# Three moves in an instruction order: a merge behind the next maximum, a norm ahead of a merge, a product begun within another

## The chip, the cores and the metric

The kernel runs on one core of one Trainium2 chip. The metric is the device time of one execution in microseconds (us), lower is better. The time before is 416.09 us, the median of 6 runs (415.14 to 417.43).

## The reference

Attention with normalised queries and keys, and behind it a two-layer network without a bias:

```python
# q, k, v: (8, 12, 448, 64) float32; w_in (768, 2048), w_out (2048, 768)
def rmsnorm(x, g):
    return x / np.sqrt(np.mean(x * x, axis=-1, keepdims=True) + 1e-06) * g
q_n, k_n = rmsnorm(q, g_q), rmsnorm(k, g_k)
scores = (q_n @ k_n.transpose(0, 1, 3, 2)) / np.sqrt(64)
scores = scores - np.max(scores, axis=-1, keepdims=True)
attn = np.exp(scores)
attn = attn / (np.sum(attn, axis=-1, keepdims=True) + 1e-09)
x = (attn @ v).transpose(0, 2, 1, 3).reshape(3584, 768)
h = x @ w_in
out = np.maximum(0.01 * h, h) @ w_out
```

## The kernel before

**Units.** The attention is cut into 24 units `u`, each of four heads of one batch entry; three units make one batch entry `b` (448 tokens). A unit has four steps `d` = 0 to 3, each with one or two of its seven score tiles `t`. In a step TensorE (PE) makes the scores (`qk`, L199), ScalarE (ACT) takes their exponential (`ex`, L218), and PE multiplies with v one unit later (`pv`, L367, with the sums `zcol`, L307).

**The shift.** One constant per unit is subtracted inside the exponential. At `d` = 0 VectorE (DVE) takes the maximum of the first score tile (`shift_max`, L236) and multiplies it into a diagonal `dg` (L238). PE spreads it over the partitions with two small matmuls (`shift_mm`, L248). DVE reduces that (L249) to the bias `eb` (L257). The matmuls stand in PE's order behind the `pv` and `zcol` matmuls of the unit before; their result lies in the same PSUM tile as that unit's `pv`, which ACT copies out after L249 (`pv_out`, L322). Then come the exponential and on PE the items of the network.

**The norm of a later unit.** At `d` = 2 of unit `u`, unit `u + 2` is normalised: ACT makes `rinv` (L164, L165), DVE multiplies q by it and then k (`prep_norm`, both L171: `n<-rq`, `n<-rk`), and a transposing DMA on SP's queue (L183) reads the result.

**The product on GpSimd.** In some units `attn @ v` times 1/sum is taken on GpSimd (POOL): `xmul_pool`, L347, `xt<-x,rz`. It waits for `rz`, which four DMAs on SP's queue (L337) spread over the partitions.

**The network.** Its work is a list of items, `queue`, filled once per batch entry (`push`). A step pops as many items as the table `PLAN` says. Between items `fill` runs small pieces of attention work, the `jobs` of the step, one behind each item. First-layer items (`moe1`, L389) make 128 of the 2048 hidden features and end with the leaky ReLU on ACT (L383). Most second-layer tiles are made two at a time with Strassen's scheme, seven products instead of eight (`seven`, items `i0` to `i6`, all matmuls at L476). Each product is eight matmuls into a PSUM bank: `ma`, `mb`, `mc`, `md`. Two of them are used twice: the sixth product (`i5`) adds into `mc`, the seventh (`i6`) into `md`, each after DVE has read what the third-bank and fourth-bank products (`i3`, `i4`) left there. DVE merges the products into the output tile `ost` (`add`, L483; the first is a copy, L496), and `put` stores it through SP's queue (L409). The operands `sa` are sums of hidden features that DVE makes (`s1` to `s4`, L457 to L466).

**Order.** There is no scheduler: each engine runs its instructions in the order in which the Python code issues them. A merge isn't issued with its product but put on the list `pend` by `later`; the next item's `flush` issues what is on the list. At the end of a step `flush(keep=...)` issues it too, but may keep the sums `s1` to `s4` for the next step. `i4` carries a mark `merges`: behind it `fill` runs no job at `d` = 2, so that the norm doesn't stand before the merge of `i4`.

A group of seven products ends exactly at `d` = 3 of units 9, 12, 15, 18 and 21. There `i3` and `i4` lie in `d` = 2, `i5` and `i6` in `d` = 3, and the next unit's maximum follows.

**The tail.** Behind the attention come the last batch entry's items. The last group but one of seven products is `mixed`: its `sa` sums are made in two halves of four of the eight blocks, the second halves only when the last hidden features are there. So its `i0` makes six matmuls of `ma`, four of `mb` (first half of `sa` 1), and the last two of `ma`; `i1` makes the other four of `mb`.

Of the kernel before, what the change touches and what calls it, by code (L numbers as in the profile page):

```python
# [18 lines left out]
def kernel(  # L19
# [37 lines left out]
    def aux(shape, dtype, name):  # L57
        if held:
            return held[0].pop(0)
        return psum.tile(shape, dtype, tag="aux", bufs=4, name=name)  # L60
# [6 lines left out]
    def drop(bank):  # L67
        if held:
            held[0].append(bank)
# [24 lines left out]
    HF = FT // 2  # L94
    HC = DM // 2
    tw = cst.tile([P, 4, HF, HC], FP16)
    sa = cst.tile([P, 4, HF, P], FP16)
# [302 lines left out]
    def col(t):  # L400
        return 64 * (5 - 2 * t) if t < 3 else P * (t - 3)

    def store(pair, t, tile_, c, last):
        for y in range(2):
            n = 2 * t + (1 - y if t < 3 else y)
            b, grp = 2 * pair + n // NS, n % NS
            dst = out[b * S:(b + 1) * S, :].rearrange("(p t) m -> p t m", t=NS)
            eng = nc.scalar if last and y else nc.sync
            eng.dma_start(dst[:, grp, c], tile_[64 * y:64 * y + 64, c])  # L409

    ost = {}
    pend = []
    L, R, LR = slice(0, HC), slice(HC, DM), slice(0, DM)

    def flush(keep=False):
        kept = [p for p in pend if keep and p[0] in (s1, s2, s3, s4)]
        now = [p for p in pend if p not in kept]
        pend[:] = kept
        for fn, args in now:
            fn(*args)  # L420

    def out_tile():
        return opool.tile([P, DM], FP32, tag="ost", name="ost")

    def moe2(pair, t, half, part, late=False):
        flush()
        if half == 0 and part == 0:
            ost[0] = out_tile()
        if part == 0:
            ost[1] = aux([P, 512], FP32, "op2")  # L430
        op2 = ost[1]
        fts = (0, 1, 2, 3, 4, 5, 8, 9, 10, 12, 13, 11, 14, 15, 6, 7) if late else range(FT)
        for i in range(8 * part, 8 * part + 8):
            ft = fts[i]
            nc.tensor.matmul(op2[:, 0:HC], gt[:, ft, ds(col(t), P)], wout16[:, ft, ds(HC * half, HC)],  # L435
                             start=(i == 0), stop=(i == FT - 1))
        if part == 0:
            return
        nc.vector.tensor_copy(ost[0][:, ds(HC * half, HC)], op2[:, 0:HC])
        drop(op2)  # L440
        if half == 1:
            store(pair, t, ost[0], LR, False)

    def wblock(i, j):
        return wout16[:, HF * i:HF * i + HF, HC * j:HC * j + HC]
# [7 lines left out]
    def gblock(t, j):  # L453
        return gt[:, HF * j:HF * j + HF, ds(col(t), P)]
# [13 lines left out]
    def later(fn, *args):  # L468
        pend.append((fn, args))

    def seven(pair, tt, nxt=None, last=False, mixed=False):
        g = {}

        def mm(bank, a, b, first, fs=range(HF)):
            for f in fs:
                nc.tensor.matmul(bank[:, 0:HC], a[:, f], b[:, f], start=(first and f == 0), stop=(f == HF - 1), skip_group_check=not first)  # L476

        def bank(name):
            g[name] = aux([P, 512], FP32, name)
            return g[name]  # L480

        def add(dst, src, name):
            nc.vector.tensor_tensor(dst, g[name][:, 0:HC], src, op=ALU.add)  # L483

        def put(i, c):
            store(pair, tt[i], g["o"][i], c, last)

        def i0():
            flush()
            g["o"] = (out_tile(), out_tile())  # L490
            ma = bank("ma")
            if mixed:
                mm(ma, gblock(tt[0], 0), wblock(0, 0), True, range(6))
                mm(bank("mb"), sa[:, 1], tw[:, 1], True, range(4))
            mm(ma, gblock(tt[0], 0), wblock(0, 0), True, range(6 if mixed else 0, HF))
            later(lambda: nc.vector.tensor_copy(g["o"][1][:, L], g["ma"][:, 0:HC]))  # L496

        def i1():
            flush()
            mm(g["mb"] if mixed else bank("mb"), sa[:, 1], tw[:, 1], True, range(4 if mixed else 0, HF))  # L500
            later(lambda: add(g["o"][1][:, L], g["o"][1][:, L], "mb"))
            later(lambda: drop(g["mb"]))

        def i2():
            flush()
            mm(g["ma"], gblock(tt[0], 1), wblock(1, 0), False)
            later(lambda: nc.scalar.copy(g["o"][0][:, L], g["ma"][:, 0:HC]))
            later(lambda: drop(g["ma"]))
            if last:
                later(put, 0, L)  # L510

        def i3():
            flush()
            mm(bank("mc"), sa[:, 0], tw[:, 0], True)
            later(lambda: add(g["o"][1][:, R], g["o"][1][:, L], "mc"))
            if nxt:
                later(s1, nxt)

        def i4():
            flush()  # L520
            mm(bank("md"), sa[:, 2], tw[:, 2], True)
            later(lambda: add(g["o"][1][:, R], g["o"][1][:, R], "md"))
            if last:
                later(put, 1, R)

        i4.merges = True

        def i5():
            flush()
            mm(g["mc"], sa[:, 3], wblock(1, 1), False)  # L530
            if nxt:
                later(s2, nxt)
            later(lambda: add(g["o"][0][:, R], g["o"][1][:, L], "mc"))
            later(lambda: drop(g["mc"]))
            later(put, 0, R if last else LR)
            if nxt:
                later(s3, nxt)
                later(s4, nxt)

        def i6():  # L540
            flush()
            mm(g["md"], gblock(tt[1], 1), tw[:, 3], False)
            later(lambda: add(g["o"][1][:, L], g["o"][1][:, L], "md"))
            later(lambda: drop(g["md"]))
            later(put, 1, L if last else LR)

        return [i0, i1, i2, i3, i4, i5, i6]

    HK = KT // 2
# [191 lines left out]
    def fill(u, d, jobs):  # L741
        for n in range(int(PLAN[u - 3][d])):
            fn = queue.pop(0)[1]
            fn()
            if jobs and not (d == 2 and hasattr(fn, "merges")):
                jobs.pop(0)()
        flush(keep=d == 3 and u < NU - 1)
        for job in jobs:
            job()
# [21 lines left out]
    with tc.manual_schedule():  # L771
# [191 lines left out]
        for u in range(3, NU):  # L963
            for d in range(4):
# [24 lines left out]
                jobs = []  # L989

                def job(fn, *args):
                    jobs.append(lambda: fn(*args))
# [58 lines left out]
                if d == 3 and 6 <= u < NU - 3:  # L1051
                    for ti in range(2):
                        job(prep_sq, u + 3, ALL, (ti,))
                fill(u, d, jobs)
        zsum_slot(NU - 1)
        pv(NU - 1)
        zinv(NU - 1)
        xmul(NU - 1, (0,))
        for i, more in enumerate((((xmul, NU - 1, (1,)), (x_sum, B - 1, 3), (x_sum, B - 1, 1)), ((x_sum, B - 1, 2), (x_sum, B - 1, 4)))):
            c, fn = queue[i]  # L1060
# [33 lines left out]
```

## Time and profile before

| | us |
|---|---|
| median of 6 runs | 416.09 |
| lowest, highest run | 415.14, 417.43 |
| the profiled execution | 416.73 |
| its span (first to last instruction) | 414.9 |
| PE busy in it | 399.8 |
| DVE busy | 309.4 |
| ACT busy | 300.2 |
| POOL busy | 68.9 |

A row of the busy time by stretches has the stretch, its length, and then for PE, PE's weight loads, DVE, ACT and POOL the busy time and in brackets the number of instructions; then the granted TensorE clock (1.00 is full speed), the DMA engines' share and GB/s. A row of the order of time has the start and the duration in us, the engine, the line, the operation, `output<-inputs`, shapes and count, and in square brackets how long the engine sat idle before it and what ended that. Matmuls are pipelined: a row of eight matmuls of 384 columns is 1.46 us long, but the next product starts 1.30 us after it.

### The profile page before, as it was taken

Reading aid. Unit: us, or ns where it says so; the run is one execution under the profiler, and the core shown is the slowest. Engines: PE = TensorE matmul, PEld = TensorE weight load, DVE = VectorE, ACT = ScalarE, POOL = GpSimd, SP = SyncE. Lnnn points to the kernel's source line nnn. Section 1 sums busy time; section 2 is a strip of 40 time slices with the busy share of each in tenths; the row PEclk is TensorE's granted clock in tenths of the full one; section 3 lists DMA queues with packets and bytes.
Section 4 is the critical chain, followed back from the end, with each engine's and each line's share of the span. In section 5 each row is a group of like instructions: output and inputs, shape, how many; then the busy total and the mean of one; then the engine's idle time right before and its main releaser. Section 6 shows DMA issues by size and latency. Waiting matters only on the chain.

```text
span 414.9 us, 9374 instructions
## 1 busy us (share of the span) xinstructions
PE 399.8 (96%) x3831; PEld 219.8 (53%) x3831; DVE 309.4 (75%) x492; ACT 300.2 (72%) x470; POOL 68.9 (17%) x70
## 2 busy tenths in 40 slices
PE   8789999999999999999999999998999999999995
PEld 7455444554445544554445544454445557558863
DVE  5888798998788666767669757766768788658762
ACT  5898987677887699686987779866986657653600
POOL 1868432200020200020020100003002202000000
PEclk9899999999999999999999999999999999999999
DMA  6999999899665895678664795676662470032023
GB/s 203 277 236 253 240 250 163 214 177 207 136 155 96 222 236 91 154 174 185 154 154 75 211 214 131 171 155 122 201 112 47 120 148 20 8 78 76 2 56 98
DMA packets 71951, 62.41 MB, mean 150 GB/s; under 512 B 36325, under 2 KB 67045, under 8 KB 71909
## 3 DMA queue, kind: packets, MB, share of 16 engines
q1 hardware_dynamic: 61312, 49.62, 47.1%
q0 software_dynamic: 10272, 11.80, 18.2%
q8 instruction: 30, 0.49, 0.5%
q10 hardware_dynamic: 324, 0.39, 0.3%
q14 instruction: 13, 0.10, 0.1%
HBM read 45.61 MB, written 11.01 MB: 136 GB/s over the span
## 4 chain that ended last, share of the span: by engine, by line
PE 81%; DVE 9%; ACT 4%; issue 2%; DMA 2%; SPq 1%; DVEq 0%; ACTq 0%
PE hps L389 27%; PE sT L199 9%; PE op L435 5%; PE sT L367 5%; PE bank L602 5%; PE bank L476 5%; PE ma L476 5%; PE mc L476 4%; PE md L476 4%; DVE n L171 4%; ACT et L218 3%; PE mb L476 2%; PE zc L307 2%; PE sT L476 1%; DVE sT L236 1%
## 5 line engine op out<-in xcount | busy, mean ns | idle before, releaser
L218 ACT ACTIVATE et<-sT,eb 128x896 f16<-128x896 f32 x166 | 159.7, 1010 | 24.6 <-PE sT L199 14.6
L389 PE MATMUL hps<-xt,win 128*128 128x448 f16 x600 | 120.8, 353 | 0.2 <-DVE xt L376 0.2
L389 PEld LDWEIGHTS <-win 128*128 128x128 f16 x612 | 56.7, 98 | 58.3 <-issue 9.5
L383 ACT ACTIVATE gt<-hps 128x448 f16<-128x448 f32 x100 | 54.0, 557 | 4.7 <-PE hps L389 4.1
L199 PE MATMUL sT<-qkT 64*64 64x448 f16 x664 | 53.1, 367 | 2.8 <-ACT et L218 2.1
L159 DVE TENSOR_REDUCE ssq<-sq 128x14 f32<-128x896 f32 (+2 forms) x49 | 50.1, 1059 | 0.4 <-ACT sq L148 0.3
L476 PEld LDWEIGHTS <-sa 128*128 128x128 f16 x352 | 32.8, 98 | 26.4 <-issue 5.8
L128 POOL DMA_DIRECT2D vt<-in_v_dram x24 | 17.9, 746 | 168.3 <-PE sT L367 162.2
L322 ACT COPY x<-sT 128x896 f32<-128x896 f32 x16 | 14.5, 907 | 31.9 <-DVE sT L249 31.9
L476 PEld LDWEIGHTS <-gt 128*128 128x128 f16 x264 | 25.3, 98 | 18.4 <-issue 2.1
L199 PEld LDWEIGHTS <-qkT 64*64 64x64 f16 x672 | 15.4, 104 | 35.4 <-issue 31.3
L347 POOL TENSOR_TENSOR xt<-x,rz 128x896 f16<-128x896 f32 x9 | 19.4, 2154 | 82.8 <-DMA rz<-zs 82.8
L171 DVE TENSOR_TENSOR n<-rq,rinv 128x896 f16<-128x896 f32 (+2 forms) x25 | 27.5, 1105 | 3.4 <-ACT rinv L165 3.4
L236 DVE TENSOR_REDUCE sT<-sT 128x1 f32<-128x896 f32 x22 | 24.1, 1094 | 7.4 <-PE sT L199 7.3
L367 PE MATMUL sT<-et,vt 64*64 64x448 f16 x532 | 28.4, 349 | 0.0
L435 PE MATMUL op<-wout,gt 128*128 128x384 f16 x160 | 28.4, 327 | 0.0
L171 DVE TENSOR_TENSOR n<-rk,rinv 128x896 f16<-128x896 f32 (+2 forms) x26 | 28.1, 1085 | 0.0
L292 DVE TENSOR_TENSOR ea<-ea,et 128x896 f16<-128x896 f16 x27 | 16.9, 625 | 13.6 <-ACT et L218 12.4
L367 PEld LDWEIGHTS <-vt 64*64 64x64 f16 x672 | 20.2, 107 | 10.7 <-issue 0.4
L435 PEld LDWEIGHTS <-gt 128*128 128x128 f16 x192 | 17.7, 98 | 13.7 <-issue 3.1
L476 PE MATMUL ma<-wout,gt 128*128 128x384 f16 x128 | 23.5, 326 | 0.0
L148 ACT ACTIVATE sq<-rq 128x896 f32<-128x896 f32 (+2 forms) x18 | 16.3, 913 | 1.2 <-DMA rq<-in_q_dram 1.2
(144 smaller groups left out, 543.8 us busy)
## 6 DMA issues: line engine op xcount, KB each, us to landing
rq<-in_q_dram SPq DMA_DIRECT2D x24, 448.0 KB, 3.9
rk<-in_k_dram SPq DMA_DIRECT2D x24, 448.0 KB, 5.1
out_dram<-ost SPq DMA_DIRECT2D x52, 192.0 KB, 3.3
rz<-zs SPq DMA_DIRECT2D x76, 112.0 KB, 2.3
vt<-in_v_dram POOLq DMA_DIRECT2D x24, 224.0 KB, 4.7
win<-in_moe_w_in_dram POOLq DMA_DIRECT2D x8, 384.0 KB, 14.8
wout<-in_moe_w_out_dram POOLq DMA_DIRECT2D x2, 1536.0 KB, 28.6
out_dram<-ost SPq DMA_DIRECT2D x4, 96.0 KB, 2.1
```

The costliest lines, as they stand in the source:

```text
L159: nc.vector.tensor_reduce(buf(u, "ssq")[:, ti, :, c[0]:c[1]], buf(u, f"sq{ti}")[:, :, c[0]:c[1]], axis=AXL.X, op=ALU.add)
L171: nc.vector.tensor_tensor(buf(u, "n16")[:, ti, c[0]:c[1]].rearrange("p s a d -> p a s d"), src[:, :, c[0]:c[1]], buf(u, "rinv")[:, ti, :, ...
L199: nc.tensor.matmul(banks[a][64 * r:64 * r + 64, 0:S].rearrange("p (t x) -> p t x", t=NS), kT(u, r, a, t), qT(u, r, a), start=True, stop=True)
L218: nc.scalar.activation(s["et"][:, t], sT[:, :, 0:S], AF.Exp, bias=s["eb"], scale=1.0)
L236: nc.vector.tensor_reduce(s["spare"][:, 511:512], sT[:, :, 0:S], axis=AXL.XY, op=ALU.max)
L347: eng.tensor_tensor(xts[b][:, g], s["x32"], s["rz"], op=ALU.mult)
L367: nc.tensor.matmul(s["pv"][r][64 * a:64 * a + 64, 0:S], vts[u % NV][64 * r:64 * r + 64, a, t], s["et"][64 * r:64 * r + 64, t, a], start=(t ...
L383: nc.scalar.activation(dst, src, AF.Prelu, bias=0.0, scale=1.0, alpha=0.01)
L389: nc.tensor.matmul(hps[:, 0:S], win16[:, kt // 2, kt % 2, ts(ft, P)], xt[:, kt // 2, kt % 2], start=(kt == 0), stop=(kt == KT - 1))
L435: nc.tensor.matmul(op2[:, 0:HC], gt[:, ft, ds(col(t), P)], wout16[:, ft, ds(HC * half, HC)], start=(i == 0), stop=(i == FT - 1))
L476: nc.tensor.matmul(bank[:, 0:HC], a[:, f], b[:, f], start=(first and f == 0), stop=(f == HF - 1), skip_group_check=not first)
L602: nc.tensor.matmul(bank[:, HX * i:HX * i + HX].rearrange("p (t x) -> p t x", t=NS), w, x[:, kt], start=start, stop=(kt == HK - 1), skip_gr ...
```

## The change

It has three parts. The merge of `i6`, with the release of its bank and the store, becomes one function `end` with the mark `waits`; the `flush` at the end of a step with `keep` keeps such a function, so that it is issued by the next flush, which stands behind `shift_max` of the next unit. The rule that no job follows `i4` at `d` = 2 now holds in unit 12 alone, so that in units 9, 15, 18 and 21 the norm of q is issued before the merge of `i4`. And in the `mixed` group, `i0` takes a bank for `mc` and makes the first four matmuls of the fourth product (`i3`) at its end.

```diff
     def flush(keep=False):
-        kept = [p for p in pend if keep and p[0] in (s1, s2, s3, s4)]
+        kept = [p for p in pend if keep and (p[0] in (s1, s2, s3, s4) or hasattr(p[0], "waits"))]
@@ i0
             mm(ma, gblock(tt[0], 0), wblock(0, 0), True, range(6 if mixed else 0, HF))
+            if mixed:
+                mm(bank("mc"), sa[:, 0], tw[:, 0], True, range(4))
@@ i3
-            mm(bank("mc"), sa[:, 0], tw[:, 0], True)
+            mm(g["mc"] if mixed else bank("mc"), sa[:, 0], tw[:, 0], True, range(4 if mixed else 0, HF))
@@ i6
-            later(lambda: add(g["o"][1][:, L], g["o"][1][:, L], "md"))
-            later(lambda: drop(g["md"]))
-            later(put, 1, L if last else LR)
+            def end():
+                add(g["o"][1][:, L], g["o"][1][:, L], "md")
+                drop(g["md"])
+                put(1, L if last else LR)
+
+            end.waits = True
+            later(end)
@@ fill
-            if jobs and not (d == 2 and hasattr(fn, "merges")):
+            if jobs and not (d == 2 and u == 12 and hasattr(fn, "merges")):
```

The same instructions are issued as before. ACT, POOL and SP keep their order; DVE's order changes at the ends of the five units, PE's in the `mixed` group.

## The prediction

> **What bounds the kernel now.** I read the first page, then the busy time by stretches, then the order of time where a stretch has a hole.
>
> ```profile
> PE 399.8 (96%) x3831; PEld 219.8 (53%) x3831; DVE 309.4 (75%) x492; ACT 300.2 (72%) x470; POOL 68.9 (17%) x70
> ...
> PE 81%; DVE 9%; ACT 4%; issue 2%; DMA 2%; SPq 1%; DVEq 0%; ACTq 0%
> ```
>
> TensorE (PE) is busy 96% of the span and is 81% of the chain that ended last. A change to VectorE (DVE) pays only where PE stands still for it. So: where does PE stand still? The stretches from 60 us to 391.9 us answer it:
>
> ```profile
> 185.00:192.50 7.50, 6.62 (x90) 3.79 (x87) 6.36 (x9) 4.30 (x5) 2.39 (x2) 1.00 0.78 145
> 192.50:232.00 39.50, 39.50 (x339) 19.48 (x338) 29.17 (x47) 31.55 (x53) 3.80 (x4) 1.00 0.64 150
> ...
> 280.30:288.50 8.20, 6.83 (x91) 3.87 (x88) 6.88 (x9) 4.50 (x6) 3.51 (x2) 1.00 0.57 117
> ```
>
> The second number is PE's busy time. PE is full everywhere (the middle line is one of the full ones, the rest has 0.2 us of holes in all) but for 0.88 us at the end of unit 12 and 1.37 us at the end of unit 18. The waits name both: matmul L248 (`shift_mm`) waits for `dg` of the next unit's maximum. In unit 18, DVE's order of time is:
>
> ```profile
> 278.65 0.56 DVE L483 TENSOR_TENSOR ost<-mc,ost 128x384 f32<-128x384 f32 x1 [0.66 <-PE mc L476]
> 279.95 0.56 DVE L483 TENSOR_TENSOR ost<-md,ost 128x384 f32<-128x384 f32 x1 [0.74 <-PE md L476]
> 280.43 1.08 DVE L171 TENSOR_TENSOR n<-rq,rinv 128x896 f16<-128x896 f32 x1
> 281.43 2.98 DVE L171 TENSOR_TENSOR n<-rk,rinv 128x896 f16<-128x896 f32 x1
> 284.33 0.55 DVE L483 TENSOR_TENSOR ost<-mc,ost 128x384 f32<-128x384 f32 x1
> 284.98 0.56 DVE L483 TENSOR_TENSOR ost<-md,ost 128x384 f32<-128x384 f32 x1
> 285.46 1.09 DVE L236 TENSOR_REDUCE sT<-sT 128x1 f32<-128x896 f32 x1
> 286.58 0.29 DVE L238 TENSOR_TENSOR dg<-ident,sT 128x128 f16<-128x128 f16 x1
> ```
>
> and beside it on GpSimd (POOL) and PE:
>
> ```profile
> 280.71 2.75 POOL L347 TENSOR_TENSOR xt<-x,rz 128x896 f16<-128x896 f32 x1 [9.60 <-DMA rz<-zs]
> ```
> ```profile
> 284.69 0.85 PE L307 MATMUL zc<-et,onesr 128*32 128x224 f16 x28
> 286.92 0.22 PE L248 MATMUL sT<-dg,onesp 128*128 128x64 f16 x2 [1.37 <-DVE dg L238]
> ```
>
> See three things. The norm of k (L171, n<-rk) takes 2.98 us instead of 1.08, because POOL's product runs beside it (280.71 to 283.46) and the norm ends 0.95 us after POOL does; in unit 12 the norm of q ends 187.58, again 0.95 after POOL's 186.63. Both products' last merges (L483, of mc and md) then stand before the maximum L236. And the maximum's scores were ready at 283.44: all of its lateness is DVE's queue. Unit 12 shows the same with 0.88 us:
>
> ```profile
> 188.51 0.55 DVE L483 TENSOR_TENSOR ost<-mc,ost 128x384 f32<-128x384 f32 x1
> 189.16 0.56 DVE L483 TENSOR_TENSOR ost<-md,ost 128x384 f32<-128x384 f32 x1
> 189.63 1.09 DVE L236 TENSOR_REDUCE sT<-sT 128x1 f32<-128x896 f32 x1
> ```
>
> The chain suggests a 448 KB load of rq ahead of the norm at 280.43. I don't believe it: that load, issued at 276.90, is unit 22's, the norm is unit 20's, and the norm starts when the md merge before it lets go.
>
> The third hole is in the tail, in the last-but-one group of seven products:
>
> ```profile
> 394.20 0.82 PE L476 MATMUL sT<-tw,sa 128*128 128x384 f16 x4 [0.16 <-DVE sa L460]
> 394.86 1.46 PE L476 MATMUL bank<-wout,gt 128*128 128x384 f16 x8
> ```
>
> **The change part by part.** No instruction is added or removed; ACT, POOL and SP keep their order. DVE's order changes at the ends of five units (9, 12, 15, 18, 21), PE's at one place.
>
> *A: seventh product's merge behind the next maximum.* At the five ends the order becomes mc merge, maximum, dg, md merge, L249. The maximum has no wait for the merge, so it starts one step (0.48 us, from the md merge's start to the maximum's start) after the mc merge. Unit 12: 188.51 + 0.48 = 188.99 instead of 189.63, 0.64 us earlier. PE's matmul can begin 0.79 us after the zc matmuls begin (144.09 to 144.87 where nothing waits), that is at 189.36 + 0.79 = 190.15; dg lets it begin at 191.09 - 0.64 = 190.45. Gain 0.64.
>
> What queues behind the moved merge is L249 and eb, and so the copy of x and the first exponential on ACT. In units 9, 15, 21 DVE idles 0.70 us before L249 (145.14 in unit 9) and the merge takes 0.56, so it fits. In units 12 and 18 the idle time is 0.31, so L249 comes 0.17 to 0.34 us later relative to PE (start to start 0.48, or 0.65 where the next waits for the result; I take 0.25). Cover: the exponential in unit 18 ends at 289.38, and PE needs the freed bank for the scores at 290.5, behind 18 matmuls. 1.1 us of cover, cost zero; without it at most 0.34 twice. SP's two stores of this tile stand behind the merge: in unit 9 they go out at about 144.9 instead of 143.1 at the earliest, four of them end by 146.6 now, and SP's next issue is L337 at 148.37. Hidden. The md bank is freed later, but its next user is the third hps product, over 2 us after the L248 matmul.
>
> *B: norm of q ahead of the fourth product's merge in units 9, 15, 18, 21.* Unit 18: rinv is done at 279.50; with the hand-over of L249 to ACT (0.08) the norm of q starts 279.58, ahead of POOL's 280.71. Step to the next 1.00: md merge at 280.58, norm of k at 281.06. POOL now need not wait for the norm of q and runs 280.71 to 282.79 (its 2.08 of eight of nine instances). The norm of k ends 282.79 + 0.95 = 283.74 instead of 284.41: 0.67 earlier. With A's order: mc merge 283.66, maximum 284.14, dg 285.26, L248 at 285.60 instead of 286.92. PE could go at 284.69 + 0.79 = 285.48, so this is the whole hole but 0.12: gain 1.32 with A, of which A is 0.65 and B 0.67.
>
> Who waits for the delayed md merge? PE's seventh product adds into the md bank and may not begin before the merge has read it. Unit 18: merge done about 281.1, product at 281.66. Unit 9: rinv 138.89, norm 138.97, merge 139.97 to 140.5, product at 141.06. Units 15 and 21: the same 0.5 us to spare. No cost. There is no gain in 9, 15, 21 either: PE has no hole there.
>
> Here a rule of the Trainium skill speaks against B. SBUF, "Who interferes with whom": a DVE operation with two SBUF inputs (the norm) and a GpSimd operation that reads SBUF exclude each other for a whole instruction, first come first served, while a DVE operation with one SBUF input (a merge: the other is PSUM) doesn't take part. The 2.98 and 2.75 us rows agree, and so does the 0.56 us mc merge at 138.05 beside POOL. By the rule B opens a gap: during the md merge at 280.58 nobody holds the port, POOL takes it at 280.71, and the norm of k still waits. Unhindered, that norm would end at 282.1 and PE would gain 1.44; the rule and the rows make it 1.32. I take 1.32.
>
> *C: fourth of the last seven products begins within the second.* Four matmuls (sa0 by tw0, first half, written long before at 386.38) move ahead of the second half of mb, which waits for L460 (393.72 to 394.15). The two ma matmuls begin at 393.56; at 1.30/8 = 0.163 each the next could start at 393.89, and started about 394.21 (394.86 less 0.65). The four fill 393.89 to 394.54, past L460. The hole by the profile's idle column is 0.16, by the starts 0.32. Perfetto Trace Analysis, "Identifying the Most-Contended Engine", says that busy time of pipelined matmuls is no good measure[...]. I take 0.32: what follows is PE back to back to 410.46, so the starts decide. DVE's later operands are early enough (s3 at 395.0 against its product at 397.1).
>
> Sum: 0.64 + 1.32 + 0.32 = 2.28 us. The profiled execution took 416.73 (span 414.9 and 1.83 around it), so it would be 414.45; it lies 0.64 above the median of 416.09. From the median: **413.8 us**, 0.55% less. A measurement of this kernel can tell about 0.3%, 1.25 us, from no change.
>
> **The rivals.**
>
> *1. The port goes the other way in unit 18 (chance 0.15).* POOL starts when rz lands: 6.45 us after its first issue (274.26) here, 5.62 in unit 12, 4.30 to 4.50 in the other seven. If it lands over 1.13 us earlier, the norm of q waits for POOL, the md merge is done about 283, PE's product stalls 1.35 us, and L248 comes at 286.9 as before: unit 18 gives nothing. Left: 0.64 + 0.32, so 415.1. For it: the spread of landings. Against: the DMA load of that stretch is the program's own. The reverse, rz later, would take the hole out of the kernel before too, to the same 415.1.
>
> *2. The holes close elsewhere (0.11).* The late eb, or a load that arrives by its own clock, takes back what the maximum gives: 416.0. Against: full PE for 36 us and more behind each hole.
>
> *3. Slower (0.08).* In units 9, 15, 21 the norm of q loses the port instead, as POOL comes late there. The md merge then holds up PE's seventh product. It decides from rz landing 5.5 us after its first issue (4.3 to 4.5 now): POOL would start at 137.47 in unit 9, the merge end 141.06. With unit 18's 6.45 the stall is 0.95 us in each, 2.85 in all, less 0.96 kept: 418.0. For it: unit 18 shows that such landings occur. Against: those three vary by 0.2 us.
>
> **How the numbers follow.** Chances: forecast 0.66 (its own range 413.0 to 414.8), rival 1 0.15, rival 2 0.11, rival 3 0.08. The range 412.9 to 415.9 goes from all three holes closed, starts counted (0.94 + 1.44 + 0.32 = 2.7 and half a microsecond of spread), to past rival 1. Faster by over 0.3% (below 414.84) 0.68, the forecast and a little of rival 1; same 0.24; slower (above 417.34) 0.08.
>
> **What would show it.** Right: L248's wait for dg gone or under 0.3 us in both units; in unit 18 a norm of q at about 279.6, POOL 2.08 long, norm of k ending about 283.7; PE full at the tail's mb. Wrong: a norm of q of over 2 us, an L476 md product that waits for the merge, or a new PE hole after L249.

## The result, and the profile after

The changed kernel takes 414.13 us (median of 15 runs, 413.35 to 416.92) against 416.22 us (34 runs) before; the ratio is 0.9951, with a 95% interval of 0.9937 to 0.9965. That is 2.09 us less, and the interval reaches from 1.5 to 2.6 us. The profiled execution took 414.18 us with a span of 412.4 us.

The page first: PE's share of the span and of the chain that ended last.

```profile
PE 399.5 (97%) x3831; PEld 219.7 (53%) x3831; DVE 308.2 (75%) x492; ACT 299.9 (73%) x470; POOL 68.3 (17%) x70
...
PE 87%; DVE 6%; ACT 4%; issue 1%; DMA 1%; SPq 0%; DVEq 0%
```

PE does the same work (399.5 us against 399.8) in a shorter span. The busy time by stretches (second number: PE) says where:

```profile
185.00:192.50 7.50, 7.50 (x97) 4.08 (x90) 5.80 (x9) 5.02 (x6) 1.83 (x2) 1.00 0.60 130
...
280.30:288.50 8.20, 8.20 (x98) 4.39 (x99) 6.78 (x11) 5.92 (x10) 2.35 (x2) 1.00 0.55 94
```

Both stretches are full now, and no wait of L248 for dg is left after 60 us. DVE's order of time at the end of unit 18:

```profile
277.98 0.56 DVE L483 TENSOR_TENSOR ost<-mc,ost 128x384 f32<-128x384 f32 x1 [0.66 <-PE mc L476]
278.85 1.09 DVE L171 TENSOR_TENSOR n<-rq,rinv 128x896 f16<-128x896 f32 x1 [0.31 <-ACT rinv L165]
279.86 0.55 DVE L483 TENSOR_TENSOR ost<-md,ost 128x384 f32<-128x384 f32 x1
280.33 2.51 DVE L171 TENSOR_TENSOR n<-rk,rinv 128x896 f16<-128x896 f32 x1
282.76 0.55 DVE L483 TENSOR_TENSOR ost<-mc,ost 128x384 f32<-128x384 f32 x1
283.23 1.08 DVE L236 TENSOR_REDUCE sT<-sT 128x1 f32<-128x896 f32 x1
284.34 0.29 DVE L238 TENSOR_TENSOR dg<-ident,sT 128x128 f16<-128x128 f16 x1
284.55 0.55 DVE L483 TENSOR_TENSOR ost<-md,ost 128x384 f32<-128x384 f32 x1
285.08 0.30 DVE L249 TENSOR_REDUCE sT<-sT 128x1 f32<-128x128 f32 x1
```

and POOL and PE beside it:

```profile
279.81 2.08 POOL L347 TENSOR_TENSOR xt<-x,rz 128x896 f16<-128x896 f32 x1 [9.37 <-DMA rz<-zs]
```
```profile
284.02 0.86 PE L307 MATMUL zc<-et,onesr 128*32 128x224 f16 x28
284.81 0.23 PE L248 MATMUL sT<-dg,onesp 128*128 128x64 f16 x2
```

The norm of q is first and takes 1.09 us. POOL takes its 2.08 (2.75 before). The norm of k still waits for POOL and ends 282.84, 0.95 after POOL's 281.89. The maximum follows the mc merge by 0.47 us, and L248 stands 0.79 us after the zc matmuls: PE waits for nothing. At the end of unit 12 PE doesn't wait either. Before, from POOL's product to L248 (rows of DVE and PE between them left out):

```profile
184.55 2.08 POOL L347 TENSOR_TENSOR xt<-x,rz 128x896 f16<-128x896 f32 x1 [8.76 <-DMA rz<-zs]
185.10 2.48 DVE L171 TENSOR_TENSOR n<-rq,rinv 128x896 f16<-128x896 f32 x1
...
189.36 0.85 PE L307 MATMUL zc<-et,onesr 128*32 128x224 f16 x28
...
191.09 0.22 PE L248 MATMUL sT<-dg,onesp 128*128 128x64 f16 x2 [0.88 <-DVE dg L238]
```

and after:

```profile
184.00 2.07 POOL L347 TENSOR_TENSOR xt<-x,rz 128x896 f16<-128x896 f32 x1 [7.96 <-ACT et L218]
...
185.36 1.67 DVE L171 TENSOR_TENSOR n<-rq,rinv 128x896 f16<-128x896 f32 x1
...
187.95 0.54 DVE L483 TENSOR_TENSOR ost<-mc,ost 128x384 f32<-128x384 f32 x1
188.49 1.10 DVE L236 TENSOR_REDUCE sT<-sT 128x1 f32<-128x896 f32 x1
...
189.62 0.85 PE L307 MATMUL zc<-et,onesr 128*32 128x224 f16 x28
...
190.41 0.23 PE L248 MATMUL sT<-dg,onesp 128*128 128x64 f16 x2
```

But here POOL also came earlier than before: 0.62 us after the start of `i4` (183.38), against 1.43 us (183.12). (`i4` is the product that fills bank md; the prediction calls it the fourth.) That isn't the change's doing: this time varies from 0.55 to 1.32 us over the seven profiles with part A and from 0.57 to 1.43 over the four without. The difference was there already when SP issued the four DMAs that spread `rz`; the issues took 3.69 us before (first row) and 2.91 us after (second row):

```profile
178.93 3.69 SPq L337 DMA_DIRECT2D rz<-zs  x4
179.19 2.91 SPq L337 DMA_DIRECT2D rz<-zs  x4
```

The tail, PE's order of time:

```profile
391.46 0.49 PE L476 MATMUL bank<-wout,gt 128*128 128x384 f16 x2
391.78 1.46 PE L476 MATMUL sT<-tw,sa 128*128 128x384 f16 x8
393.08 1.46 PE L476 MATMUL bank<-wout,gt 128*128 128x384 f16 x8
394.38 0.81 PE L476 MATMUL sT<-tw,sa 128*128 128x384 f16 x4
395.03 1.46 PE L476 MATMUL bank<-tw,sa 128*128 128x384 f16 x8
```

The row of eight at 391.78 is the first half of mc and the second half of mb in one run, without a wait. From the first ma matmul (389.83) to the first md matmul (395.03) are 5.20 us; before, 391.93 to 397.46, 5.53.

A balance of the two profiles, by starts on PE. The first ma matmul of the first group of seven comes 0.25 us later than before (118.97 against 118.72), which is nothing that the change touched. L248 of unit 12's end comes 0.68 us earlier (190.41 against 191.09), that of unit 18's end 2.11 earlier, the tail's first ma matmul 2.10 earlier, and the last merge 2.43 earlier (408.23 against 410.66). So between these two profiles unit 12 gave 0.93, unit 18 gave 1.43, the tail 0.33. The 0.93 is not the work of part A alone: POOL's earlier start is in it.

### The profile page after: what moved, and what is told of

It reads as the page before. It is cut to its first block, busy times and chain, and to the rows that moved or that the text cites. A ratio compares the mean times of both kernels' runs of the same rounds, so it can differ in the third digit from the quotient of the medians.

```text
span 412.4 us, 9369 instructions
## 1 busy us (share of the span) xinstructions
PE 399.5 (97%) x3831; PEld 219.7 (53%) x3831; DVE 308.2 (75%) x492; ACT 299.9 (73%) x470; POOL 68.3 (17%) x70
## 4 chain that ended last, share of the span: by engine, by line
PE 87%; DVE 6%; ACT 4%; issue 1%; DMA 1%; SPq 0%; DVEq 0%
PE hps L389 27%; PE sT L199 9%; PE sT L367 6%; PE op L435 6%; PE mc L476 5%; PE ma L476 5%; PE bank L476 5%; PE md L476 5%; PE bank L608 5%; PE zc L307 3%; PE mb L476 3%; ACT et L218 2%; DVE n L171 2%; PE sT L476 2%; PE bank L435 1%
## 5 line engine op out<-in xcount | busy, mean ns | idle before, releaser
L476 PEld LDWEIGHTS <-sa 128*128 128x128 f16 x352 | 32.8, 98 | 26.0 <-issue 5.8
L476 PEld LDWEIGHTS <-gt 128*128 128x128 f16 x264 | 25.3, 98 | 18.4 <-issue 2.1
L476 PE MATMUL ma<-wout,gt 128*128 128x384 f16 x128 | 23.5, 327 | 0.0
L292 DVE TENSOR_TENSOR ea<-et 128x896 f16<-128x896 f16 x14 | 9.4, 673 | 11.3 <-ACT et L218 11.3
```

Source lines behind the costliest of these rows:

```text
L292: nc.vector.tensor_tensor(s["ea"], s["et"][:, 0] if t == 1 else s["ea"], s["et"][:, t], op=ALU.add)
```

## The experiments

Below, a hole is counted from where PE could go on: L248's start less the start of the zc matmuls less 0.79 us. So the kernel before has holes of 0.94 us (unit 12) and 1.44 us (unit 18) in its profile. The kernel before was measured again beside each group of versions: its median was 416.22 us beside the changed kernel, 416.10 beside e1 to e4, 415.84 beside e5 to e8 and 415.79 beside e9 and e10. A fall is counted from the median measured beside it; where two versions of different groups are compared, their ratios are compared too.

**Each part alone.** Part A (e1_merge_only), from the kernel before:

```diff
-        kept = [p for p in pend if keep and p[0] in (s1, s2, s3, s4)]
+        kept = [p for p in pend if keep and (p[0] in (s1, s2, s3, s4) or hasattr(p[0], "waits"))]
...
+            end.waits = True
+            later(end)
```

> Part A alone (merge of the seventh product behind the next maximum, at five ends); norm of q and the tail as before. Theory of the holes: time follows from PE's two holes alone. Unit 12 as in the changed kernel: the maximum starts one step (0.48 us) after the mc merge instead of 1.12 us, hole 0.94 -> 0.30 or less; unit 18: 1.44 -> 0.79, as the norm of k still ends 0.95 us after POOL's product. Sum -1.29 us, about 414.9 us. Rival (the merge between dg and L249 delays the bias, and PE pays behind it): L249 comes 0.17 to 0.34 us later after L248 and a new PE hole follows; about 415.6 us.

Measured: 414.63 us against 416.10, ratio 0.9968 (0.9959 to 0.9977), 1.47 us less. Unit 12 has no hole, unit 18 one of 0.50 (L248 at 284.76, zc at 283.47). The bias came hardly later: L249 starts 0.27 us after L248 in unit 12 and 0.34 in unit 18, against 0.26 before, and no PE hole follows. POOL was first in unit 18 here (278.89, the norm of q 279.21 and 2.71 us long), so the hole that A met was smaller than 1.44; e3 below shows its size.

Part B (e2_norm_only):

```diff
-            if jobs and not (d == 2 and hasattr(fn, "merges")):
+            if jobs and not (d == 2 and u == 12 and hasattr(fn, "merges")):
```

> Part B alone (norm of q ahead of the fourth product's merge in units 9, 15, 18, 21). Theory of the holes: only unit 18 gains, since its norm of q runs before POOL's product instead of delaying it: POOL 2.08 us instead of 2.75, norm of k ends 0.67 us earlier, hole 1.44 -> 0.77; unit 12 keeps 0.94. About 415.55 us. Rival (the delayed merge holds up PE's seventh product, which adds into the same bank): L476 md waits at 0.1 to 1 us in up to four units; 416.2 to 418 us.

Measured: 415.23 us, ratio 0.9985 (0.9978 to 0.9993), 0.87 us less. Unit 18's hole is 0.53, no L476 waits for a merge. Unit 12, which B doesn't touch, had a hole of only 0.08 in this profile: POOL began 0.57 us after `i4`'s start (1.43 in the kernel before) and was done early. So the rival of the held-up product falls. And a hole in unit 12 follows POOL's start. In the four profiles that have the old order there (the kernel before, e3, e7, e2) POOL began 1.43, 1.22, 0.86 and 0.57 us after `i4`'s start, and the holes were 0.94, 0.73, 0.35 and 0.08: about half a microsecond less each time. POOL's start in turn follows SP: in all eleven profiles with this product (e5 leaves it out) the four issues of rz took 2.83 to 3.69 us, and POOL's start after `i4`'s was that time less 2.26 to 2.29 us.

Part C (e3_product_only):

```diff
+            if mixed:
+                mm(bank("mc"), sa[:, 0], tw[:, 0], True, range(4))
...
-            mm(bank("mc"), sa[:, 0], tw[:, 0], True)
+            mm(g["mc"] if mixed else bank("mc"), sa[:, 0], tw[:, 0], True, range(4 if mixed else 0, HF))
```

> Part C alone (four matmuls of the fourth product between, in the tail). By the starts of matmuls the tail gets 0.32 us shorter (first ma matmul of that group to the first md matmul: 5.53 -> 5.20 us); by the profile's idle column 0.16. Time 415.9 us, within what can be told from no change. Units 12 and 18 keep their holes of about 0.9 and 1.4 us: this run shows also how these vary from one profile to the next.

Measured: 415.35 us, ratio 0.9985 (0.9974 to 0.9995). The tail's stretch is 5.20 us (392.95 to 398.15): 0.33 saved, as the starts said and not the idle column. The time itself fell by 0.75, whose interval (0.2 to 1.1) holds 0.33 and does not say more. The holes in this profile are 0.73 and 1.15 us.

In unit 18 this profile and that of part A make a pair that shows what A is worth. POOL was first in both and began 1.65 and 1.66 us after `i4`'s start. In the old order (e3):

```profile
281.40 2.08 POOL L347 TENSOR_TENSOR xt<-x,rz 128x896 f16<-128x896 f32 x1 [8.98 <-DMA rz<-zs]
...
287.94 0.22 PE L248 MATMUL sT<-dg,onesp 128*128 128x64 f16 x2 [1.09 <-DVE dg L238]
```

and with A (e1):

```profile
278.89 2.08 POOL L347 TENSOR_TENSOR xt<-x,rz 128x896 f16<-128x896 f32 x1 [8.99 <-DMA rz<-zs]
...
284.76 0.22 PE L248 MATMUL sT<-dg,onesp 128*128 128x64 f16 x2 [0.44 <-DVE dg L238]
```

The wait falls from 1.09 to 0.44 us: 0.65 us, the predicted step.

**B in unit 12 as well** (e4_norm_in_12_too), from the changed kernel:

```diff
-            if jobs and not (d == 2 and u == 12 and hasattr(fn, "merges")):
+            if jobs:
```

> The changed kernel with part B in unit 12 as well (the exemption taken away). In unit 12 rinv is ready about 0.1 to 0.3 us from POOL's start, so who has the port first is nearly a toss. If the norm of q is first: norm 1.08 us, merge in time, POOL waits about 1 us, the norm of k ends as late as now: no hole, 414.1 us as the changed kernel. If POOL is first: the norm takes about 2.6 us, the md merge ends 0.8 us after PE wants to begin the seventh product, an L476 md wait of about 0.9 us appears: about 415.0 us. Rival (order doesn't matter, the port is always won by the one that was issued first): 414.1 us.

Measured: 414.97 us, ratio 0.9975 (0.9966 to 0.9983); 0.84 us slower than the changed kernel's 414.13, 1.0 us by the ratios. POOL won by 0.05 us. POOL, DVE and PE in this run:

```profile
184.29 2.07 POOL L347 TENSOR_TENSOR xt<-x,rz 128x896 f16<-128x896 f32 x1 [8.35 <-DMA rz<-zs]
```
```profile
184.34 2.97 DVE L171 TENSOR_TENSOR n<-rq,rinv 128x896 f16<-128x896 f32 x1 [0.31 <-ACT rinv L165]
187.23 0.54 DVE L483 TENSOR_TENSOR ost<-md,ost 128x384 f32<-128x384 f32 x1
```
```profile
187.83 1.46 PE L476 MATMUL md<-tw,gt 128*128 128x384 f16 x8 [1.19 <-DVE ost L483]
```

Read it from the bottom: PE's seventh product waits 1.19 us for the merge, the merge for the norm, and the norm (2.97 us, ending 0.95 after POOL) for the port. So the exemption of unit 12 is worth most of a microsecond where POOL is first.

**POOL's product taken away** (e5_no_pool_read), from the kernel before:

```diff
+        if u in (11, 17):
+            nc.gpsimd.memset(xts[b][:, g], 0.0)
+            return
         eng.tensor_tensor(xts[b][:, g], s["x32"], s["rz"], op=ALU.mult)
```

> The kernel before, with POOL's product of units 11 and 17 replaced by a POOL memset of the same tile: it writes and reads nothing, and x of these two units is zero (that part of the computation is left out). It takes away what both norms collide with at the ends of units 12 and 18, and leaves every order as it was. Theory of the port: both norms take 1.08 us there, the two merges stay ahead of the maximum and L248 waits for dg in neither unit; -0.94 and -1.44 us, about 413.8 us, without any of the three parts. Rival (the merges ahead of the maximum make the hole by themselves): holes of 0.5 us and more stay; 415 us or more.

Measured: 414.07 us, ratio 0.9955 (0.9938 to 0.9971). The memset ran from 175.46 and from 269.86, 0.86 us long, so POOL did nothing beside the norms. DVE and PE at unit 18's end, in the old order:

```profile
280.17 1.08 DVE L171 TENSOR_TENSOR n<-rk,rinv 128x896 f16<-128x896 f32 x1
281.17 0.55 DVE L486 TENSOR_TENSOR ost<-mc,ost 128x384 f32<-128x384 f32 x1
281.90 0.56 DVE L486 TENSOR_TENSOR ost<-md,ost 128x384 f32<-128x384 f32 x1 [0.18 <-PE md L479]
282.38 1.09 DVE L236 TENSOR_REDUCE sT<-sT 128x1 f32<-128x896 f32 x1
```
```profile
284.22 0.23 PE L248 MATMUL sT<-dg,onesp 128*128 128x64 f16 x2
```

Both norms take 1.08 us, both merges stand before the maximum as they always did, and PE has no hole in either unit. The rival falls: the merges ahead of the maximum make no hole by themselves. The cause of the holes is the collision of the norms with POOL's product; the change doesn't remove it but makes room behind it. What in the product collides, its reads or its writes, this run doesn't separate. The time fell by 1.77 us (1.2 to 2.6), less than the 2.38 of the two holes in the profile of the kernel before. That fits with what the old order shows on the average: unit 12's hole is 0.53 us over its four profiles, unit 18's 1.34 over three (the kernel before, e3 and e7).

**A late POOL in units 9, 15 and 21** (e6_after_pool_twice, from the changed kernel; e7_before_pool_twice, from the kernel before):

```diff
-        eng.tensor_tensor(xts[b][:, g], s["x32"], s["rz"], op=ALU.mult)
+        for n in range(2 if u in (8, 14, 20) else 1):
+            eng.tensor_tensor(xts[b][:, g], s["x32"], s["rz"], op=ALU.mult)
```

> The changed kernel, with POOL's product of units 8, 14 and 20 made twice in a row, so that POOL holds the port at the ends of units 9, 15 and 21 for 2.08 us longer, as a late rz would (rival 3 of the prediction). Theory: the norm of q, first in the queue now, takes about 2.7 us and ends about 0.95 us after POOL; the md merge behind it ends about 1.0 us after PE wants to begin the seventh product: three L476 md waits for L483 of about 1.0 us, 414.1 + 3.0 = 417.1 us. Rival (the merge has slack enough, or PE doesn't wait for it): 414.1 to 414.5 us.

> The kernel before with the same doubled product in the same three units. Theory: the md merge is ahead of the norm of q and PE's seventh product doesn't wait; the norms end late and L248 waits for dg about 0.2 us in each of the three units: 416.1 + 0.6 = 416.7 us, so that the kernel before and the changed one are about level under a late POOL. Rival (a late POOL costs both the same): 416.1 + 3 = 419 us.

Measured: the changed kernel 417.09 us (ratio to the kernel before 1.0029, 1.0020 to 1.0038), the old order 416.62 us (1.0014, 1.0004 to 1.0023). Unit 9's end in the changed kernel, DVE and PE:

```profile
138.80 2.73 DVE L171 TENSOR_TENSOR n<-rq,rinv 128x896 f16<-128x896 f32 x1 [0.31 <-ACT rinv L165]
141.46 0.54 DVE L484 TENSOR_TENSOR ost<-md,ost 128x384 f32<-128x384 f32 x1
```
```profile
142.06 1.46 PE L477 MATMUL md<-tw,gt 128*128 128x384 f16 x8 [0.95 <-DVE ost L484]
```

and in the old order:

```profile
139.93 0.56 DVE L484 TENSOR_TENSOR ost<-md,ost 128x384 f32<-128x384 f32 x1 [0.74 <-PE md L477]
140.40 1.83 DVE L171 TENSOR_TENSOR n<-rq,rinv 128x896 f16<-128x896 f32 x1
```
```profile
145.74 0.22 PE L248 MATMUL sT<-dg,onesp 128*128 128x64 f16 x2 [0.22 <-DVE dg L238]
```

The same POOL costs the changed kernel 0.95, 0.92 and 0.78 us in units 9, 15 and 21, at the product. It costs the old order a wait of 0.22 us in unit 9, at the maximum, and holes of 0.5 us in the three units together. Rival 3 is a real mechanism; it did not come about since POOL is early in these units (in the kernel before it begins 1.38 us ahead of `i4` in unit 9: 136.47 against 137.85).

**B in unit 18 alone** (e8_norm_in_18_only, from the changed kernel, and e9_18_only_pool_twice with the doubled product):

```diff
-            if jobs and not (d == 2 and u == 12 and hasattr(fn, "merges")):
+            if jobs and not (d == 2 and u != 18 and hasattr(fn, "merges")):
```

> The changed kernel with part B in unit 18 alone (the exemption holds in 9, 12, 15 and 21). Theory: PE has no hole in 9, 15 and 21 either way, so the time is that of the changed kernel, 414.1 us, and all of B's gain is unit 18's. Rival (an earlier norm and transpose of k help a later step in those units too): slower than the changed kernel by 0.3 us or more.

> The version with part B in unit 18 alone (A and C as in the changed kernel), with POOL's product of units 8, 14 and 20 made twice as in the two runs before. Theory: in 9, 15 and 21 the md merge is ahead of the norm of q again, so PE's seventh product doesn't wait, and with A the maximum comes 0.5 us earlier than in the kernel before, which closes its 0.2 us holes there too: 414.1 to 414.4 us, against 417.1 for the changed kernel under the same POOL. Rival (the doubled product costs by itself, not by the merge behind the norm): 416.5 us or more.

Measured: 414.15 us (0.9957, 0.9942 to 0.9973), the changed kernel's time. With the doubled product 413.83 us (0.9954, 0.9942 to 0.9967): a late POOL costs this version nothing that can be measured, against 3 us for the changed kernel, and no PE hole is left in units 9, 15 and 21. In units 9, 15 and 21 B brings nothing and is a risk. This version isn't faster than the changed kernel, but it is the one to keep.

**A and C without B** (e10_no_norm_move: the rule behind `i4` in all units, the rest as changed):

> Parts A and C without B. What B adds when A is there: unit 18 keeps the rest of its hole, 0.3 to 0.8 us by when rz lands; everything else as in the changed kernel. 414.4 to 414.9 us against 414.1. Rival (A closes both holes alone): 414.1 us.

Measured: 414.60 us (0.9970, 0.9958 to 0.9982). POOL, DVE and PE in unit 18:

```profile
279.77 2.08 POOL L347 TENSOR_TENSOR xt<-x,rz 128x896 f16<-128x896 f32 x1 [9.17 <-DMA rz<-zs]
```
```profile
279.92 2.88 DVE L171 TENSOR_TENSOR n<-rq,rinv 128x896 f16<-128x896 f32 x1
```
```profile
285.65 0.22 PE L248 MATMUL sT<-dg,onesp 128*128 128x64 f16 x2 [0.61 <-DVE dg L238]
```

Here POOL was ahead of the norm of q by 0.15 us, and both norms ran after it. A without B leaves a hole of 0.68 us in unit 18 (0.50 in e1); the time is 0.47 us above the changed kernel's, 0.8 by the ratios, in line with it though the intervals of the two overlap. In unit 12 POOL began 1.32 us after `i4`'s start, nearly as late as in the kernel before, and the hole was 0.17. The old order would have had about 0.82 there: an estimate, half a microsecond less than POOL's start as in its four profiles. So A took about 0.65 us in unit 12 too.

## Why the prediction was right, point by point

Forecast 413.8, measured 414.13 us; the forecast fall of 2.28 us was 2.09 by the medians and 2.55 by the profiled executions. The mechanism was right in all three parts; the depth of the holes was taken from one profile, and here the nearness of the two numbers is in part luck.

- *Where PE stands still.* Right for the profile that was read: three holes, and no others opened. All three are closed. But their depth changes from execution to execution, and this profile had the latest POOL of all eleven in both units, counted from `i4`'s start: 1.43 us in unit 12 (0.55 to 1.32 in the others), 2.26 us in unit 18 (1.45 to 2.06). With the old order's holes that these starts would give, and A worth 0.65 at most, an estimate for the usual execution is 0.4 in unit 12, 1.3 in unit 18 and 0.33 in the tail: 2.0 us, near the 2.09 measured.
- *Unit 12, 0.64 us.* The step is right, and e10 shows it where POOL is late. But the 0.93 between the two profiles is mostly rz: POOL began 0.62 us after `i4`'s start instead of 1.43, and the norm of q was 1.67 us long instead of 2.48. At such a start the old order too would leave only about 0.13 (0.08 in e2, at 0.57). In the usual execution 0.64 is too large.
- *Unit 18, 1.32 us.* The profile gave 1.43, all there was. The order of events was as written: the norm of q ahead of POOL, POOL 2.08 us, the norm of k 0.95 us behind it, which waited because POOL had begun (279.81) by the time the md merge stood between the norms (279.86). The merge took its usual 0.55 us beside POOL, as the rule cited in the prediction has it. POOL began 0.23 us earlier after `i4`'s start than in the profile before, and so the last 0.12 us of the hole went too.
- *The split of unit 18 into 0.65 and 0.67.* Right for A: 0.65, by e3 and e1. With A in place B took what was left, 0.50 to 0.68 (e1, e10). B's gain has two forms. In the kernel before and e7 POOL came second, and the norm of k waited for it, as the prediction says. In e1, e3 and e10 POOL came first, and the norm of q waited. The parts alone fell by 1.47, 0.87 and 0.75 us, 3.1 in all, more than together (2.09); each fall is known to 0.3 to 0.4 us only, so the excess is not established.
- *The tail, 0.32 us.* Measured 0.33. Reading starts rather than the idle column (0.16) was the right choice. The section cited for it speaks of how close a kernel is to the roofline, not of holes; that the starts decide here is shown by 5.53 and 5.20 us.
- *L249 0.17 to 0.34 us later, hidden.* Too large. Where PE still waited for dg, L249 came 0.33 or 0.34 us after L248 (e1 and e10) instead of 0.26: 0.08 later at most. The merge starts 0.21 us after dg's start (284.34, 284.55), not at dg's end. In the changed kernel, where PE is the later one, it is 0.27. No PE hole follows it.
- *The md merge is read in time.* Right, with 0.5 us to spare: in unit 18 it starts at 279.86 and the product at 280.99 without a wait. How thin that is, e4 and e6 show.
- *Rival 1.* It did not happen in any profile with B in unit 18; the nearest POOL came 0.37 us after the norm of q had begun (278.74 and 279.11 in e9), and then POOL was the one to wait, 2.66 us long. In the kernels without B it did happen that POOL was first (e1, e3, e10), since the norm of q stands 0.9 us later there (1.98 us after `i4`'s start instead of 1.07). That is what B gains: it moves the norm out of POOL's way.
- *Rival 2.* Not seen: unit 18's L248 is 2.11 us earlier than before and the tail's first ma matmul 2.10, so nothing was taken back between them.
- *Rival 3.* Not in the ordinary runs; its price of 0.78 to 0.95 us per unit and its place were shown by e6.

Two things stay open. What makes the issues of rz in unit 12, and its landing in unit 18, longer in one execution than in another was not tried. And single runs of one kernel differ by up to 3.7 us (415.08 to 418.80 in the kernel before), profiles in the first 120 us by up to 1.8 us (the first ma matmul at 118.43 in e1, 120.23 in e3). The granted clock goes with this. In the changed kernel the ten runs with a mean clock of 0.999 or 1.000 took 413.35 to 414.51 us, the five with 0.989 to 0.996 took 414.18 to 416.92. In e3's profile the clock is 0.88 from 10 to 20 us and 0.78 from 20 to 30 us, in e1's 1.00 in both. In the profiles of the kernel before and of the changed one it is the same in these two stretches (0.89 and 0.94), so the balance above is not touched. No run set the clock, so that it is the cause is not shown.

## What to carry to other kernels

When one engine is nearly full, look for the few stretches where it isn't, and follow the wait there to the queue behind it; a reordering on another engine is worth exactly that hole, and nothing in the places that have none. Read the depth of the hole in several executions before it goes into a sum: unit 12's was 0.94, 0.73, 0.35 and 0.08 us in four. Before an operation is moved ahead of another, ask what the one that is passed over releases: here a merge that frees an accumulator is safe behind a norm only as long as the norm isn't held up itself. Make the move only in the places where it closes a hole, since everywhere else it only spends slack.

## What was not expected of the hardware

How near a tie can be, and still decide for a whole instruction: POOL's row started 0.05 us before the norm's, and the norm ended 0.95 us after POOL's 2.07 us (e4). With the norm of q already running, POOL waited instead (2.75 us in the kernel before). And how regular it is: in all 31 cases of the eleven profiles in which a norm waited for POOL's product it ended 0.94 to 0.96 us after it.

A blocked operation is drawn as a long busy one, not as idle time: no row of waits names these collisions, and only the durations (2.97 and 2.75 us where 1.08 and 2.08 are usual) show them.
